# Loading the values of a cached attention 8 MB at a time, with 64 KB descriptors

## The chip, the cores and the metric

One core of one Trainium2 chip. The metric is the device time of one execution in microseconds; all runs below are recorded as of the fast state (none is over 1.5% above the fastest run of its kernel), but for one single run that is marked.

A *descriptor* is one contiguous piece that a DMA engine moves; in these traces each shows as one *packet* record, with its size and duration. The *span* is the time from the first to the last instruction of the profiled run.

## The reference, cut to what matters

One decode step of grouped-query attention with a long cache, beside a small gated FFN:

```python
# x: [1, 1, 448]; k_cache, v_cache: [1, 8, 65536, 256] bf16, 268 MB each
q = (layernorm(x) @ wq) ...                      # 16 query heads of 256
k, v = repeat(k_cache, 2), repeat(v_cache, 2)    # 2 query heads share a KV head
p = softmax(q @ k.T * 256 ** -0.5)
out = x + (p @ v) @ wo + ffn(layernorm(x))       # ... cut: the FFN reads some 5 MB
```

Every byte of both caches is read once: 549.03 MB in all with the weights. Almost nothing is written.

## The kernel before: the parts that matter

A ring of four slots, each 4 MB (128 partitions x 32 KB), takes all key and value blocks. One queue (SyncE) issues all loads. A block is 64 tokens of each partition; partition p holds the tokens p*512 to p*512+511 of a head, so one block is one contiguous run of 32 KB in each partition, both in HBM and in SBUF.

```python
NSLOT = 4; CH = 64; HC = 2           # 4 slots; 64 tokens per block; a unit is 2 blocks
SLOT = CH * Dh                       # 64 * 256 bf16 = 32 KB per partition
ring = S_("ring", [P, NSLOT * SLOT], BF16)

def slot_item(kd, u, c, parts=None):         # load block c of unit u, "k" or "v"
    ...
    r = rounds[0]; rounds[0] += 1
    s = r % NSLOT                            # its slot
    for k, (sem, J) in enumerate(parts or [("slot%d" % s, CH)]):
        ap = ring[:, s * SLOT + o * Dh:s * SLOT + (o + J) * Dh]
        item((kd, u, c, k), [(ap.rearrange(...),  # waits until the slot's last user is done:
                              src[0, h]...[:, n0 + o:n0 + o + J, :], sem)],
             [("FREE", r - NSLOT)] if r >= NSLOT and k == 0 else ())
# ... cut ...
for t in range(NT):                          # main loop: 28 turns
    slot_item("k", t + U, 0)                 # slot 0
    slot_item("v", t, 0)                     # slot 1
    slot_item("v", t, 1)                     # slot 2
    if t % U == 0: ...                       # every 4th turn a small weight load (wo)
    slot_item("k", t + U, 1)                 # slot 3
for t in range(NT, NU):                      # last 4 units: values only
    for c in range(HC):
        slot_item("v", t, c, last_parts(...) if ... else None)

def turn_B(t):                               # what TensorE does in a turn
    k_slots(sets_of(u, 0), s0, at)           # first K block: 4 sets of 16 transposes, q.k
    pe_V(t, 0, True, True)                   # first V block: 32 matmuls
    pe_tot(t)
    pe_V(t, 1, True, True)                   # second V block
    dve_ob(t)
    k_slots(sets_of(u, 1), s0, at)           # second K block
    ...
```

A K slot is free when its last transposes are through; a V slot when its 32 matmuls are.

## Time and profile before

| | before |
|---|---|
| median of 3 runs | 1284.51 us (1284.49 to 1285.25) |
| span of the profiled run | 1283.4 us |
| HBM read | 549.03 MB, 428 GB/s over the span |
| load queue: packets, share of 16 DMA engines | 22,210, 99.6% |
| TensorE busy | 72% |

The page of before: the span, from the slice table the DMA row (busy share of the 16 DMA engines in tenths, 40 equal slices) and what they moved, then the packet total and the load queue (packets, MB, share of 16 engines' span):

```profile
span 1283.4 us, 22878 instructions
...
DMA  9999999999999999999999999999999999999997
GB/s 405 427 433 427 433 432 431 430 431 432 432 433 431 433 430 433 430 433 430 433 432 432 432 431 432 429 433 433 431 432 432 432 430 433 431 431 433 431 429 318
DMA packets 22228, 549.22 MB, mean 428 GB/s; under 512 B 2371, under 2 KB 4422, under 8 KB 5190
...
q1 hardware_dynamic: 22210, 549.04, 99.6%
```

The DMA engines are busy from end to end, so a microsecond saved on a DMA engine is saved in the kernel, and one saved on TensorE isn't. The Trainium skill (DMA: Bandwidth & Descriptors, "Where 436 GB/s comes from") gives the ceiling of the 16 SBUF ports as 435.2 GB/s; the slices from the fifth to the last but one move 429 to 433, in the mean 432. So all that is left in the middle is about 0.7%.

The issuing queue's own waits (engine, line, what it waited for: us in total, times, longest):

```profile
SPq L776 <- PE ps_t L352: 855.3, 58, 20.9
SPq L776 <- PE ps_o L352: 182.8, 60, 18.6
```

The queue waits for free slots (K transposes, V matmuls) most of the time. That is no loss as long as work is still queued behind each issue. I call that the *margin* of a load: from its issue to the moment when the last byte queued before it has arrived, counted from the trace's packet records (all 16 engines together: when as many bytes have arrived as were queued). In the main loop, from its third turn on, it is 11.6 to 16.7 us for K, 18 to 21 us for the first V block and 24.6 to 26.5 us for the second.

One turn of TensorE before (start us, us, engine line op out<-in, count, and in brackets the idle time before it and what ended it). `ps_o<-ring` are V matmuls, `ps_t<-ring` K transposes:

```profile
518.23 1.90 PE L352 MATMUL ps_o<-ring,p_sb 128*4 128x512 bf16 x32
520.05 0.61 PE L352 MATMUL ps_m<-rowsum,ones_f 128*128 128x2 f32 x4
522.34 1.90 PE L352 MATMUL ps_o<-ring,p_sb 128*4 128x512 bf16 x32 [1.68 <-DMA ring<-in_A_v_cache_dram]
531.96 3.25 PE L352 MATMUL ps_t<-ident_f,ring 128*128 128x128 f32 x15 [7.72 <-DMA ring<-in_A_k_cache_dram]
```

TensorE waits for the data, both for V and for K: compute is hidden. Over the run:

```profile
PE ps_t L352 <- DMA ring<-in_A_k_cache_dram: 229.5, 30, 8.8
...
PE ps_o L352 <- DMA ring<-in_A_v_cache_dram: 67.0, 37, 9.4
```

### The profile page before, as it was taken

How to read it: one execution, taken by the hardware profiler on the slowest of the kernel's cores; microseconds unless marked ns; L12 is line 12 of the kernel's file. 1: busy time of each engine (PE TensorE's matmuls, PEld its weight loads, DVE VectorE, ACT ScalarE, POOL GpSimd, SP SyncE). 2: the span in 40 equal slices, each digit the busy share in tenths (PEclk: the TensorE clock that was granted, in tenths of full speed). 3: DMA queues.
4: the chain of work that ended last, by engine and by line, in shares of the span. 5: the costliest groups of instructions: out<-in, count | busy, mean ns of one | idle time of the engine just before them, and what ended most of it. 6: DMA issues, size and time to landing. Idle time of an engine off the chain costs nothing.

```text
span 1283.4 us, 22878 instructions
## 1 busy us (share of the span) xinstructions
PE 924.9 (72%) x9824; PEld 671.5 (52%) x9824; DVE 585.8 (46%) x1091; ACT 459.2 (36%) x655; POOL 4.5 (0%) x35
## 2 busy tenths in 40 slices
PE   3988766786666886666876667866668766678654
PEld 3867554465454565554654545654446544456411
DVE  4756443554344554444554445543445534455300
ACT  2645332353333443324433243432434333234300
POOL 1000000000000000000000000000000000000000
PEclk9988888998889988879888889888899887898876
DMA  9999999999999999999999999999999999999997
GB/s 405 427 433 427 433 432 431 430 431 432 432 433 431 433 430 433 430 433 430 433 432 432 432 431 432 429 433 433 431 432 432 432 430 433 431 431 433 431 429 318
DMA packets 22228, 549.22 MB, mean 428 GB/s; under 512 B 2371, under 2 KB 4422, under 8 KB 5190
## 3 DMA queue, kind: packets, MB, share of 16 engines
q1 hardware_dynamic: 22210, 549.04, 99.6%
q8 instruction: 8, 0.13, 0.0%
q14 instruction: 6, 0.05, 0.0%
q10 hardware_dynamic: 4, 0.00, 0.0%
HBM read 549.03 MB, written 0.00 MB: 428 GB/s over the span
## 4 chain that ended last, share of the span: by engine, by line
DMA 68%; PE 31%; SPq 0%; ACT 0%; issue 0%; DVE 0%
DMA ring<-in_A_k_cache_dram 63%; PE ps_t L352 24%; PE ps_q L352 5%; DMA w_area<-in_B_w_down_dram 3%; DMA ring<-in_A_v_cache_dram 2%; PE ps_s L352 1%; PE ps_m L352 1%; SPq L776 0%; ACT s L430 0%; DVE res_bf L727 0%; PE ps_o L352 0%
## 5 line engine op out<-in xcount | busy, mean ns | idle before, releaser
L352 PE MATMUL ps_t<-ident_f,ring 128*128 128x128 f32 x4096 | 568.8, 296 | 248.6 <-DMA ring<-in_A_k_cache_dram 229.5
L406 DVE COPY kt_buf<-ps_t 128x1024 bf16<-128x1024 bf16 x768 | 489.5, 683 | 420.9 <-PE ps_t L352 420.4
L352 PEld LDWEIGHTS ps_t<-ident_f,ring 128*128 128x128 f32 x4096 | 494.9, 152 | 354.2 <-DMA ring<-in_A_k_cache_dram 245.5
L408 ACT ACTIVATE kt_buf<-ps_t 128x1024 bf16<-128x1024 bf16 x256 | 261.9, 1023 | 356.1 <-PE ps_t L352 355.8
L430 ACT ACTIVATE s<-ps_q 98x512 bf16<-98x512 f32 x256 | 152.7, 597 | 288.1 <-PE ps_q L352 288.1
L352 PE MATMUL ps_o<-ring,p_sb 128*4 128x512 bf16 x2048 | 132.6, 401 | 67.0 <-DMA ring<-in_A_v_cache_dram 67.0
L352 PE MATMUL ps_q<-kt_buf,q_cur 128*2 128x512 bf16 x2048 | 166.2, 402 | 0.0
L352 PEld LDWEIGHTS ps_o<-ring,p_sb 128*4 128x4 bf16 x2048 | 47.7, 86 | 133.2 <-issue 75.5
L352 PEld LDWEIGHTS ps_s<-sel_bf,s 128*128 128x128 bf16 x1024 | 60.7, 99 | 54.1 <-ACT s L430 50.7
L540 DVE CAST ob_sb<-ps_o 100x512 bf16<-100x512 f32 x29 | 20.0, 691 | 142.8 <-PE ps_o L352 142.8
L352 PE MATMUL ps_s<-sel_bf,s 128*128 128x8 bf16 x1024 | 64.4, 169 | 22.6 <-ACT s L430 22.6
L497 ACT ACTIVATE p_sb<-S_sb 128x128 bf16<-128x128 bf16 x64 | 18.9, 307 | 136.2 <-PE ps_o L352 136.0
L576 DVE TENSOR_TENSOR rowsf<-ps_m,rowsf 1x448 f32<-1x448 f32 x28 | 17.1, 612 | 53.8 <-PE ps_m L352 53.8
L352 PEld LDWEIGHTS ps_q<-kt_buf,q_cur 128*2 128x2 bf16 x2048 | 27.1, 79 | 10.2 <-issue 5.0
L512 DVE RECIPROCAL rs<-ps_m 128x4 f32<-128x4 f32 x29 | 5.3, 182 | 52.8 <-PE ps_m L352 52.8
L352 PE MATMUL ps_m<-wo_cur,oT_sb 128*1 128x448 bf16 x112 | 25.7, 352 | 0.0
L352 PEld LDWEIGHTS ps_m<-rowsum,ones_f 128*128 128x128 f32 x116 | 15.1, 190 | 12.6 <-issue 12.6
L352 PE MATMUL ps_m<-rowsum,ones_f 128*128 128x2 f32 x116 | 17.6, 256 | 0.0
L352 PEld LDWEIGHTS ps_m<-wo_cur,oT_sb 128*1 128x1 bf16 x112 | 9.3, 83 | 13.5
L454 DVE CAST S_sb<-ps_s 128x256 bf16<-128x256 f32 x32 | 12.9, 404 | 4.3 <-PE ps_s L352 4.3
L487 ACT ACTIVATE S_sb<-S_sb,negmax 128x512 bf16<-128x512 bf16 x16 | 13.4, 864 | 3.6 <-DVE negmax L481 3.6
L456 DVE TENSOR_REDUCE m1p<-S_sb 128x2 f32<-128x256 bf16 x32 | 13.5, 421 | 1.1
(79 smaller groups left out, 138.3 us busy)
## 6 DMA issues: line engine op xcount, KB each, us to landing
ring<-in_A_k_cache_dram SPq DMA_DIRECT2D x64, 4096.0 KB, 25.0
ring<-in_A_v_cache_dram SPq DMA_DIRECT2D x62, 4096.0 KB, 32.0
ring<-in_A_v_cache_dram SPq DMA_DIRECT2D x2, 2048.0 KB, 28.1
w_area<-in_A_wq_dram SPq DMA_DIRECT2D x1, 3584.0 KB, 11.3
wo_cur<-in_A_wo_dram SPq DMA_DIRECT2D x7, 448.0 KB, 15.4
ring<-in_A_v_cache_dram SPq DMA_DIRECT2D x2, 1024.0 KB, 30.2
ring<-in_A_v_cache_dram SPq DMA_DIRECT2D x4, 512.0 KB, 31.4
w_area<-in_B_w_gate_dram SPq DMA_DIRECT2D x1, 1568.0 KB, 38.6
```

Of the source, the lines that this page charges most:

```text
L352: return pe.matmul(*a, **k)
L406: O(e, ("EV", s, m), lambda it: nc.vector.tensor_copy(out=kt[:, :], in_=tb[:, :]), f"ev{m}")
L408: O(e, ("EV", s, m), lambda it: nc.scalar.activation(out=kt[:, :], in_=tb[:, :], func=ACTF.Copy), f"ev{m}")
L430: O("act", ("EVQ", s), lambda it: nc.scalar.activation(out=s2[s % 2][0:QROWS, :], in_=ps_q[0:QROWS, :], func=ACTF.Copy), "evq")
L454: O("dve", ("SCOPY", u), lambda it: nc.vector.tensor_copy(out=S, in_=ps_sn))
L456: O("dve", ("SMAX", u), lambda it: nc.vector.tensor_reduce(out=m1p[:, :, k], in_=S.rearrange("p n i -> p i n"), axis=AX.X, op=ALU.max))
L487: O("act", ("EXP", h, i), lambda it, i=i: nc.scalar.activation(out=S_sb[:, :, i], in_=S_sb[:, :, i], func=ACTF.Exp, bias=negmax[:, i:i + 1 ...
L497: O("act", ("PC", t, c), lambda it: nc.scalar.activation(out=p_sb[:, c, :, :], in_=S_sb[:, n:n + CH, :], func=ACTF.Copy), "pc")
L512: O("dve", ("RS", t), lambda it: nc.vector.reciprocal(out=rs[:, :, :], in_=ps_m[0:P, C_TOT:C_TOT + NH * rep]))
L540: O("dve", ("OB", t), lambda it: nc.vector.tensor_copy(out=ob_sb[0:OROWS, :], in_=ps_o[0:OROWS, :]))
L576: O("dve", ("RES", t), lambda it: nc.vector.tensor_tensor(out=base_f, in0=ps_m[0:1, C_BIG:C_BIG + D], in1=base_f, op=ALU.add))
```

## The change

The two V blocks of a unit are adjacent in HBM and lie in adjacent slots (1 and 2), so they can be one load of 8 MB: one run of 64 KB per partition. The intent: half as many, twice as large descriptors for the values. The price: the pair is issued only when both slots are free, and its first half is usable only when all of it is there. The matmuls stay the same.

```diff
+    def pair_item(u):
+        h, n0 = u // U, (u % U) * SBN
+        r = rounds[0]
+        rounds[0] += 2
+        s = r % NSLOT
+        assert s + 1 < NSLOT
+        ap = ring[:, s * SLOT:(s + 2) * SLOT]
+        item(("v", u), [(ap.rearrange("p (j d) -> p j d", d=Dh),
+                         A_v_cache[0, h].rearrange("(p n) d -> p n d", p=P)[:, n0:n0 + 2 * CH, :], "slot%d" % s)],
+             [("FREE", r + i - NSLOT) for i in range(2)])
+        for c in range(2):
+            items[("v", u, c)] = (r + c, [(("v", u), ap[:, c * SLOT:(c + 1) * SLOT], 0, CH)])
...
     for t in range(NT):
         slot_item("k", t + U, 0)
-        slot_item("v", t, 0)
-        slot_item("v", t, 1)
+        pair_item(t)
...
     for t in range(NT, NU):
+        if (t - NT) % 2 == 0:
+            pair_item(t)
+            continue
         for c in range(HC):
```

## The prediction

> **What bounds the kernel.** The DMA engines. The slice table has the DMA row at 9 in every slice but the last, at 430 to 433 GB/s; the queue table gives the load queue 99.6% of the 16 engines' span, 549.03 MB read. The Trainium skill (DMA: Bandwidth & Descriptors, "Where 436 GB/s comes from") puts the ceiling at 435.2 GB/s; a window of the trace (400 to 800 us) moves 432, which agrees and leaves 0.8%. The issuing queue waits for ring slots (its own waits: 855 us on K transposes, 183 us on V matmuls), but comparing each issue with the moment when the bytes queued before it are through, every load is issued early: V typically by 20 and 25.5 us, K by 12 to 16 us; the least after the start is 5.4 us (at 1228.7 us, after the FFN). Compute is hidden (PE 72% busy; it waits 230 us for K, 67 us for V).
>
> **What the change does.** 30 pairs of V blocks (28 in the main loop, 2 at the end) become one 8 MB load each: 7,680 of the 16,128 packets of 32 KB become 3,840 of 64 KB. Compute instructions are unchanged.
>
> *Gain.* Single DMA packets in the trace: 4 KB 159 ns, 8 KB 309, 16 KB 611, 32 KB 1213 (fast ends). A line through all sizes is 8.2 ns + bytes / 27.2 B per ns; that slope times 16 is the ceiling. The skill ("Why small descriptors are slow") has about 3 cycles of overhead per packet; the trace shows more, 8 ns. A 64 KB packet should take 2 x 1213 - 8 = 2418 ns. Each engine saves 240 x 8 ns = 2.0 us, and 30 semaphore packets of 9 ns = 0.3 us. Estimate: **2.3 us, all on the critical path**, because the queue never runs dry. A pair should take 19.35 us instead of 19.42.
>
> *Cost.* The first V half is usable only with the second, 9.7 us later, and the pair is issued only when both slots are free. In steady state each V half takes 1.9 us on PE, with 0.6 us between, so the pair is issued about 4.5 us after the previous pair lands, with two K loads (19.4 us) still queued: margin about 15 us. First pair: issued at 101.5 us, queue ahead lasts to 108.9, margin 7 us. Pair after the FFN: issued at about 1230.4 us, margin 3.7 us. All positive: no DMA hole. PE still has 5 us after V before K lands. The tail doesn't change.
>
> **Predicted time: 1282.3 us**, range 1280.5 to 1286. Chances: faster by over 2% 0.01, within 2% 0.95, slower 0.04. Over 2% faster is nearly impossible: at 435.2 GB/s the bytes alone take 1261.6 us, plus start and tail.
>
> **What would show it.** 64 KB packets of 2415 to 2420 ns; queue packets down by about 4,300. V's median issue to landing about 34 us (15 + 19.4). PE's wait for V grows by several us per turn, its wait for K doesn't. No DMA slice below 9 except the last.
>
> **What would make it wrong.** A 64 KB packet that runs slower than the line, or is split into two again (gain 0, about 1284.5); engines that finish unequally with coarser packets; a hole where the margin is least (around 1230 us, or near 105 us), which costs its length. If a wait that I overlooked pushes the pair's issue past 19 us after the previous landing, every turn pays and the kernel gets slower by per cent.

## The result, and the profile after

| | before | after |
|---|---|---|
| median | 1284.70 us (4 runs) | 1283.03 us (1282.19 to 1283.18, 4 runs) |
| ratio | | 0.9985, 95% interval 0.9968 to 1.0002 |
| span of the profiled run | 1283.4 us | 1281.2 us |

A ratio is the mean time of one kernel's runs over that of the other's in the same rounds, so it isn't quite the ratio of the medians. Four runs leave "no difference" just inside the interval; the first experiment repeats it with more.

The page of after, the same lines:

```profile
span 1281.2 us, 22851 instructions
...
DMA  9999999999999999999999999999999999999997
GB/s 406 424 436 424 450 426 427 431 431 439 436 438 417 437 430 441 432 430 428 432 446 426 436 424 436 430 444 430 428 428 433 441 436 430 425 435 431 434 437 310
DMA packets 17908, 549.22 MB, mean 429 GB/s; under 512 B 1891, under 2 KB 3942, under 8 KB 4710
...
q1 hardware_dynamic: 17890, 549.04, 99.5%
```

The load queue has 22,210 - 17,890 = 4,320 packets less: 3,840 of data and 480 that count the semaphores of 30 loads on 16 engines. No slice lost its 9. (The profile counts a packet's bytes in the slice in which it starts; with larger packets single slices scatter more, some above the ceiling.) The queue's own waits:

```profile
SPq L791 <- PE ps_t L367: 709.1, 55, 18.6
SPq L785 <- PE ps_o L367: 343.3, 29, 21.1
```

L785 in the second line is the wait of the pair for its two slots: 29 waits of 11.8 us in the mean in place of 60 of 3.0 us. One turn of TensorE after:

```profile
521.51 3.58 PE L367 MATMUL ps_o<-ring,p_sb 128*4 128x512 bf16 x32 [5.79 <-DMA ring<-in_A_v_cache_dram]
525.02 0.61 PE L367 MATMUL ps_m<-rowsum,ones_f 128*128 128x2 f32 x4
525.55 1.90 PE L367 MATMUL ps_o<-ring,p_sb 128*4 128x512 bf16 x32
531.13 3.04 PE L367 MATMUL ps_t<-ident_f,ring 128*128 128x128 f32 x16 [3.68 <-DMA ring<-in_A_k_cache_dram]
```

The wait for V grew from 1.68 to 5.79 us in this turn, the wait for K shrank from 7.72 to 3.68: idle time moved, none of it on the critical path. Over the run:

```profile
PE ps_o L367 <- DMA ring<-in_A_v_cache_dram: 148.3, 36, 19.1
...
PE ps_t L367 <- DMA ring<-in_A_k_cache_dram: 99.1, 30, 6.8
```

Before, these two were 67.0 and 229.5 us. The first 32 V matmuls after the pause took 3.58 us instead of 1.90; that slows TensorE (its busy time rose from 924.9 to 971.8 us) and costs nothing here but margin.

The single packet records of the two traces (the durations of one DMA packet, ns; 5th percentile, called the fast end below, median, and how many):

```
size      before                   after
 8,192 B   309   312  (268)         309   312  (267)
32,768 B  1213  1216  (16,128)     1213  1215  (8,448)
65,536 B                           2418  2422  (3,840)
```

Two packets of 32 KB take 2 x 1213 = 2426 ns, one of 64 KB takes 2418: 8 ns less.

### The profile page after: what moved, and what is told of

It is laid out like the page before. It is cut to its first block, busy times and chain, and to the rows that moved or that the text cites. A ratio compares the mean times of both kernels' runs of the same rounds, so it can differ in the third digit from the quotient of the medians.

```text
span 1281.2 us, 22851 instructions
## 1 busy us (share of the span) xinstructions
PE 971.8 (76%) x9824; PEld 668.1 (52%) x9824; DVE 584.6 (46%) x1091; ACT 459.4 (36%) x655; POOL 4.5 (0%) x35
## 3 DMA queue, kind: packets, MB, share of 16 engines
q1 hardware_dynamic: 17890, 549.04, 99.5%
## 4 chain that ended last, share of the span: by engine, by line
DMA 69%; PE 30%; SPq 0%; ACT 0%; issue 0%; DVE 0%
DMA ring<-in_A_k_cache_dram 64%; PE ps_t L367 23%; PE ps_q L367 5%; DMA w_area<-in_B_w_down_dram 3%; DMA ring<-in_A_v_cache_dram 2%; PE ps_s L367 1%; PE ps_m L367 1%; SPq L791 0%; ACT s L445 0%; DVE res_bf L742 0%; PE ps_o L367 0%
## 5 line engine op out<-in xcount | busy, mean ns | idle before, releaser
L367 PE MATMUL ps_t<-ident_f,ring 128*128 128x128 f32 x4096 | 551.1, 290 | 118.1 <-DMA ring<-in_A_k_cache_dram 99.1
L367 PEld LDWEIGHTS ps_t<-ident_f,ring 128*128 128x128 f32 x4096 | 478.4, 148 | 225.4 <-DMA ring<-in_A_k_cache_dram 118.5
L367 PE MATMUL ps_o<-ring,p_sb 128*4 128x512 bf16 x2048 | 189.5, 533 | 148.4 <-DMA ring<-in_A_v_cache_dram 148.3
L367 PEld LDWEIGHTS ps_o<-ring,p_sb 128*4 128x4 bf16 x2048 | 55.3, 104 | 253.9 <-issue 228.5
L367 PEld LDWEIGHTS ps_m<-rowsum,ones_f 128*128 128x128 f32 x116 | 21.6, 262 | 22.3 <-issue 22.3
L367 PE MATMUL ps_m<-rowsum,ones_f 128*128 128x2 f32 x116 | 24.0, 312 | 0.0
```

The lines of the kernel that those rows point to most:

```text
L367: return pe.matmul(*a, **k)
```

## The experiments

Theory A is the prediction's: every packet costs a fixed time beside its bytes, and since the engines never idle, the kernel gets all of it back. Rival B: the gain comes from 30 fewer loads and completions, or from the changed timing. Rival C: the 1.7 us are scatter. The first four kernels ran on one chip, beside 9 runs of the kernel before (1285.12 us median).

### e1_again: the changed kernel, five rounds

> The changed kernel once more, five rounds. Theory A (each packet costs a fixed 8.2 ns beside its bytes, all of it on the critical path): 2.0 to 2.3 us under the kernel before, ratio 0.9982 to 0.9985, with an interval that leaves 1 out. Rival C (the 1.7 us between the medians are scatter of the runs): ratio within 0.9995 to 1.0005.

Measured: 1282.99 us (1282.34 to 1283.00), ratio 0.9982, interval 0.9968 to 0.9996. The slowest of these five runs is 1.7 us below the fastest of the nine of before (1284.73). C falls.

### e2_one_load_32k: one load of 8 MB, packets of 32 KB again

```diff
-  eng.dma_start(fn[0], fn[1]).then_inc(...)
+  eng.dma_start(fn[0], fn[1], max_dma_last_dim=32768).then_inc(...)   # for the pairs only; cut: handing the size on
```

> Still one load of 8 MB for a pair of value blocks, same ring slots, same waits, same issue times; only its packets are 32 KB again (16,128 of 32 KB, none of 64 KB). Theory A: the gain goes, but for the 30 semaphore packets: 1284.3 to 1284.9 us, ratio to before 0.9995 to 1.0003. Rival B (the gain comes from 30 fewer loads and completions, or from the changed timing, not from the packets): the time of the changed kernel, about 1282.9 us, ratio about 0.9985. Also a test of the cost side: if waiting for both slots and the later first half cost anything, this kernel is slower than before by that much.

Measured: 1285.27 us (1285.08 to 1285.32), ratio 1.0001, interval 0.9987 to 1.0014. Its page:

```profile
span 1283.4 us, 22851 instructions
...
q1 hardware_dynamic: 21730, 549.04, 99.6%
```

The gain is gone, with everything else of the change in place: loads of 8 MB, waits for both slots, margins (11.2 us in the median against 11.7 in e1). The fastest of these five runs (1285.08 us) is 2.1 us above the slowest of e1. So it was the packets, and B falls. The same run shows that the price of the change was nothing that these runs resolve: later issue and later first half leave the kernel where it was before. It also shows no gain from 30 fewer loads (the 0.3 us predicted for the semaphore packets didn't appear: 1285.27 against 1285.12, within the scatter). So e2 came in 0.4 us above the range expected of A; a saving and a cost of a few tenths that cancel would look the same.

### e3_one_load_8k and e4_one_load_2k: smaller packets

The same edit with 8192 and 2048.

> As before, with packets of 8 KB in the 30 big loads: 1,920 packets per engine in them instead of 240. Theory A: 1,680 x 8.2 ns = 13.8 us over the changed kernel, about 1296.8 us (1295 to 1299), packets of 309 ns. Rival B: about 1282.9 us.

> As before, with packets of 2 KB in the 30 big loads: 7,680 packets per engine instead of 240. Theory A: 7,440 x 8.2 ns = 61 us over the changed kernel, about 1344 us (1340 to 1350), packets of about 83.5 ns. Rival B: about 1282.9 us. More than 1350 would say that making so many descriptors costs something of its own.

Measured: 1298.71 us (1298.62 to 1298.83), ratio 1.0105; and 1352.43 us (1351.95 to 1352.48), ratio 1.0522. The queue lines, e3 first, then e4:

```profile
q1 hardware_dynamic: 44770, 549.04, 100.0%
```

```profile
q1 hardware_dynamic: 136930, 549.04, 102.0%
```

Both are above the centre of the expected range: e3 inside its range, e4 2.4 us over it. The expectation of e4 would have taken that as a cost of making so many descriptors; the table speaks against it, as e3 with a quarter of them pays the same per packet. Set against the number of packets per engine in the 30 loads:

| packets of | per engine | median us | over e1 | per extra packet |
|---|---|---|---|---|
| 64 KB (e1) | 240 | 1282.99 | | |
| 32 KB (e2) | 480 | 1285.27 | 2.28 | 9.5 ns |
| 8 KB (e3) | 1,920 | 1298.71 | 15.72 | 9.4 ns |
| 2 KB (e4) | 7,680 | 1352.43 | 69.44 | 9.3 ns |

(The last column is "over e1" divided by the packets that an engine has more than in e1: 15.72 us / 1,680. The runs scatter by some 0.3 us, which is over 1 ns in e2's figure and under 0.2 ns in e3's.) One price per packet, over a factor of 32 in size: A stands, with 9.3 to 9.5 ns instead of the 8.2 ns that the prediction read from the durations of single packets. The durations don't settle the difference: for e3 over e1 the fast ends (309 and 2418 ns) give 13.0 us per engine, the medians (314 and 2422 ns) 21.6, and the kernel lost 15.72; in e4 the durations add up to 102.0% of the span, so records overlap. Where the last 1 ns comes from stays open.

### e5 to e7: the pair issued later on purpose

The prediction says that the later issue is free while work is queued. These kernels delay the pair until one of the four transpose sets of the K block behind the previous pair is done, and so eat the margin in steps. (e9, below, is the fourth.)

```diff
         slot_item("k", t + U, 0)
+        if t:
+            W("sp", "T", (t - 1 + U) * SETS + CSETS + LATE, TORD[-1])   # LATE = 1, 2, 3
         pair_item(t)
```

> The changed kernel with the pair issued later on purpose: it also waits for the second of four transpose sets of the K block that lands after the previous pair. By the trace of the changed kernel that is about 15.6 us after the previous pair landed, and two K loads last 19.8 us from there: the queue should still have about 4 us of work, so no cost: 1282 to 1284 us. If issue time matters by itself (no threshold), it should be slower by about 9 us x 27 turns.

> The same, waiting for the third set: about 18.3 us after the landing, plus about 1 us from an issue to its first packet, against 19.8 us of queued work. On the edge: 0 to 1 us per turn, 1282 to 1310 us.

> The same, waiting for the last set: about 21 us after the landing, plus 1 us to the first packet, against 19.8 us of queued work. The DMA engines run dry for 2 to 3 us in each of 27 turns: 1340 to 1370 us, and the pair's margin in the trace is negative by 1 to 2 us.

Measured: e5 1294.94 us (ratio 1.0077), e6 1333.04 (1.0373), e7 1382.60 (1.0759); two runs each, beside 1285.00 us of before. All three lost more than expected: e5 12 us instead of none, e6 23 us above its range, e7 13 us above its range. The DMA row of e7, whose 8s are the holes:

```profile
DMA  9999899989999899999899998998988899899997
```

And its issuing queue in two turns (start us, us):

```profile
537.15 0.33 SPq L794 DMA_DIRECT2D ring<-in_A_v_cache_dram  x1
537.52 12.97 SPq L794 DMA_DIRECT2D ring<-in_A_k_cache_dram  x2
578.44 0.33 SPq L794 DMA_DIRECT2D ring<-in_A_v_cache_dram  x1
```

41.3 us from pair to pair here (42.64 in the mean of e7), where the undelayed loop takes 39.03. Why e5 loses although every pair still had 2.9 to 4.8 us of margin, its packets say in part. The first 16 packets of 64 KB of one pair (their durations in ns, in order of start):

```
after  2420 2422 2418 2422 2418 2420 2420 2422 2422 2422 2422 2422 2422 2425 2422 2427
e5     2932 3019 3355 3300 3139 2846 2867 2418 3149 2418 2415 2434 2418 3574 2418 2418
```

In e5, 514 of the 3,840 packets of 64 KB took over 30 ns more than the 2418 of the fast end, together 9.9 us per engine; in the changed kernel 4 did, 0.1 us. Half of the 514 were among the first 16 packets of a pair. Time in which fewer than 16 packets were under way, up to the end of the last load, came to 6.3 us per engine in e5 and 2.6 in the changed kernel. Together some 13 us per engine, which is about e5's 12 us.

The margin hides that the 16 engines don't end level. Each engine closes a load with its own semaphore packet, so the trace shows when the first of them had nothing left: in e5 1.35 us after the pair's issue in the median (0.55 at least), where the margin over all bytes is 3.4; in e9, below, 3.2 us (2.36 at least); in e1 9.2. The first packet of a pair started 0.94 us after the issue at the earliest (e6 and e7), and the sixteenth 1.9 us after it in the median of e7, where nothing was queued ahead. So in e5 the first engines were at or near the end of their queue while the last were not. The 8 of e5's 27 pairs whose first engine had 2 us or more ran long by 0.10 us per engine in the mean, the 19 others by 0.47. That fits a limit of some 2 us for the engine that is through first; no run here sets that one figure alone, and why the packets run long, instead of only starting late, stays open.

### e9_late_set0: the smallest delay

The same edit with LATE = 0.

> The pair held back until the first transpose set of the K block that lands after the previous pair: about 13 us after that landing, where the changed kernel issues after 6 to 8 us. Two K loads last 19.8 us, so about 6.5 us of work should still be queued. The runs so far: no loss against the packet count at 10 to 13 us of margin, 0.44 us per turn at 3.2 to 4.8 us. Theory A with a cold start of 2 to 3 us (seen where the queue ran dry) says no cost at 6.5 us: 1282.5 to 1283.5 us. If the loss grows smoothly with the delay, some 0.2 us per turn, about 1288 us.

Measured, in six runs of before and four of this: 1282.93 us (1282.41 to 1283.13), ratio 0.9983, interval 0.9965 to 1.0001. No loss. Together (27 pairs of the main loop each; the period is from landing to landing of a pair, averaged):

| | pair issued after the previous landing, median us | margin, median (least) us | period of a turn, us | kernel, us |
|---|---|---|---|---|
| before | | V blocks 19.9 and 25.4 | 39.11 | 1285.1 |
| e2, 32 KB packets | 9.1 | 11.2 (9.5) | 39.11 | 1285.27 |
| e1, as changed | 9.2 | 11.7 (9.9) | 39.03 | 1282.99 |
| e9, set 0 | 14.9 | 5.6 (4.8) | 39.03 | 1282.93 |
| e5, set 1 | 16.7 | 3.4 (2.9) | 39.50 | 1294.94 |
| e6, set 2 | 18.8 | 0.6 (-0.7) | 40.80 | 1333.04 |
| e7, set 3 | 21.3 | -1.9 (-3.2) | 42.64 | 1382.60 |

The margin has a threshold, between 5.6 and 3.4 us in the median (3.2 and 1.35 us for the engine that is through first); above it a delay costs nothing that these runs resolve; below it each further microsecond of delay costs 0.6 to 0.7 us per turn (e5 to e6: 2.1 us later, 1.30 us longer; e6 to e7: 2.5 and 1.84). In e7 a pair took 21.6 us from issue to landing with nothing ahead of it, where in the full stream it takes about 19.35 us of the engines' time: a cold start of some 2.3 us. My expectations counted 1 us, read from the first load of the kernel (issue to first packet): that holds for the first packet in e7 (0.95 us), not for the sixteenth (1.9 us). They also took the queue to last 19.8 us from each landing (19.4 in e6 and e7) and the second set to be done 15.6 us after the landing (e5: the pair was issued after 16.7).

### e8_k_pairs_too: keys in pairs as well

```diff
     for t in range(NT):
-        slot_item("k", t + U, 0)
+        pair_item(t + U, "k")
         pair_item(t)
...
-        slot_item("k", t + U, 1)
```

> Keys in pairs of 8 MB too in the main loop: almost all packets are 64 KB, so theory A alone promises another 1.8 us. But then the four ring slots are two buffers, and a K pair can be issued only when the second K block is through, after V: K pair lands, first K block 11 us, V lands at 19.4 us and takes 6 us, second K block 11 us, issue, 1 us, 19.4 us for the next K pair: about 56 us per turn instead of 38.8, 1700 to 1850 us in all.

Measured: 1814.77 us, inside the expected range; a single run, so of unknown state, but the distance to 1285 is far beyond the scatter of these runs. The DMA row and the queue:

```profile
DMA  9996558755686668756686667765687567865598
...
q1 hardware_dynamic: 13858, 549.03, 71.0%
```

The fewest packets of all, and the engines idle 29% of the span. Four slots in two pairs leave no slot to fill while a pair is in use. The queue's waits name it: it waited 1618.6 us, in 30 waits, for the transposes of the K blocks.

```profile
SPq L785 <- PE ps_t L367: 1618.6, 30, 58.4
```

## Why the prediction was right, point by point

- **The bound.** Right. The DMA engines were busy throughout before and after, and each packet more per engine cost the kernel 9.3 to 9.5 ns, whatever the size (e2 to e4). Its "430 to 433 GB/s in every slice but the last" leaves out the first four slices (405 to 433).
- **The 64 KB packet.** Right: 2418 ns at the fast end, as predicted; the median is 2422, as the 32 KB packet's median was 1216 against 1213. It was not split, and queue packets fell by 4,320 (predicted about 4,300).
- **The gain.** 2.3 us predicted; measured 1.7 us (first runs), 2.1 (e1) and 2.2 (e9, 1285.09 to 1282.93). The sum's terms were slightly off in opposite directions: the packets are worth 2.28 us (e1 against e2) instead of 2.0, the 30 saved semaphore packets nothing that the runs resolve instead of 0.3. That the sum fits better than its two terms is luck.
- **The cost, none.** Right, by e2 and e9. The size of the margin was off: "about 15 us" was 10.0 to 15.9, with a median of 12.2. The mis-sized term is the time from landing to the next issue, 4.5 us predicted and 7.6 us measured in the median of the changed kernel (9.2 in e1). It took each V block as 1.9 us on TensorE, but after the longer pause the first one took 3.58 us, in some turns both; and it left out the time from the last packet to the first matmul (0.6 us in the turn shown, whose last packet ended at 520.92 us). V's median time from issue to landing was 32.4 us for the same reason, not 34. The margin after the FFN was predicted as 3.7 us and was 4.9; a pair at 1188.8 us, which the prediction doesn't list, had 4.8. By e5 that is close to where a load begins to cost, and a single late load of e5's kind cost about 0.4 us (12 us / 27).
- **What was not tested.** Whether the 4.8 and 4.9 us near the FFN cost a few tenths has no run of its own. The trace speaks against it: the changed kernel's four long packets all lie before 240 us, and from 1185 to 1260 us the time with fewer than 16 packets under way was 0.07 us per engine, as before the change (0.08).

No kernel tried here is faster than the changed one (e9's 1282.93 us is the same time).

## What to carry to other kernels

Where DMA engines are busy from end to end, count packets: each costs a fixed time (here about 9.4 ns) beside its bytes, so going from 32 to 64 KB for the values bought 0.17% while going down to 2 KB cost over 5%. The larger load was free as long as it was issued early enough: compute its margin against the bytes still queued, and against the engine that is through first, and keep some 5 us of it, not zero (here 5.6 us cost nothing and 3.4 us did). And buy packet size only with slots that the stream can spare: here the same step for the keys halved the number of buffers and cost 41%.

## What the Trainium skill lacked or had wrong

- DMA: Bandwidth & Descriptors, "Why small descriptors are slow": about 3 cycles of overhead per packet. If they are cycles of the 850 MHz that the page gives for the fabric, that is an estimate of 3.5 ns (the 32 bytes of descriptor metadata that it names beside them would add about 1 ns, by the same estimate at 32 bytes a cycle); the durations here show 8.2 ns and the kernel's time 9.3 to 9.5 ns per packet, the same from 2 KB to 64 KB.
- The same page, "Where 436 GB/s comes from": its warning says that for transfers between HBM and SBUF the HBM side (about 358 GB/s) binds. Taken alone that misleads: with this one core running, the load stream held 429 to 433 GB/s, and the slope of the packet durations (27.2 B per ns and engine) is the 435 GB/s of the ports. The page isn't at odds with that elsewhere: it keeps the 358 for two cores of a pair that both stream, and has 425 GB/s for one.
- The same page, "Rules for kernel authors", asks for at least 1 MiB per DMA, and its measured table, of DMAs issued from GpSimd, still gains up to 16 MB. It has nothing on large loads queued one behind the other so that the queue never runs dry: 8 MB instead of 4 MB with equal packets changed nothing (ratio 1.0001).
- No page says how far ahead a load must be queued: here a margin of 5.6 us (median) was free and one of 3.4 us cost 0.4 us per load, with packets that ran up to 1.6 us longer (4,064 ns where 2,418 is the fast end) and engines that were through 1.35 us after the issue.
